# Gated linear attention feeding a top-1 mixture of experts on one core: index writes, weight splits, logits, warm products and the expert stage's order rearranged

## The chip, the core and the metric

The kernel runs on one core of one Trainium2 chip. The core has five engines with an instruction stream each: TensorE (PE, matrix products and transposes), VectorE (DVE), ScalarE (ACT), GpSimd (POOL) and SyncE (SP, which here issues most transfers). Sixteen DMA engines move data between memory and the on-chip buffers. The metric is the time of one execution in device microseconds.

## What is computed

```python
for t in range(768):                       # batch 4, 8 heads, head size 48
    state = alpha[:, :, t, :, None] * state + einsum('bhd,bhe->bhde', k_t, v_t)
    y_t = einsum('bhd,bhde->bhe', q_t, state)
x = y.transpose(0, 2, 1, 3).reshape(4, 768, 384)
logits = x @ w_gate                        # 8 experts
local = sigmoid(x @ w_local)
e = argmax(logits) if first token or local < 0.5 else expert of the token before
out = softmax(logits)[e] * (relu(x @ w1[e]) @ w2[e])     # 384 -> 1024 -> 384
```

There are 3072 tokens. Each goes through one expert alone, so the tokens of an expert are gathered by lists of indices.

## The kernel before

**Recurrence.** The tokens are cut into 24 blocks of 128 (six per sequence, the four sequences in turn), each block into two chunks of 64. Per block i, DVE runs two scans of the gates (`scan1`, tile A; `scan2`, tile sf), POOL multiplies q and k by them, PE transposes k (`kt`, kp), forms the scores (`pm`, pe), the state update (`um`, up) and the output (`ym`, y), then transposes the output (`xt`, xp) and computes the logits (`logit`, lg). DVE adds the state (`sums`, `carry`) and masks the scores; ACT copies the state (`first`, sb), kp, y (XR) and xp out of the accumulators. SP loads a, k, q three blocks ahead and v (vt) two ahead, and writes XR to memory (xd), from where experts gather tokens.

**Routing.** `route` is a generator, one per group of blocks (`SPANS`: groups of 8, 4, 8 and 4 blocks). It is stepped by `other()`, three times per block. Its DVE and PE steps find each token's expert, weight and row in the expert's list; its last steps write the rows (tile pl) to the lists in memory (ls) by indirect writes on POOL, one per block of tokens, 24 in all. A `yield` after every second write hands out two writes per call.

**Experts.** Products are made at float32 accuracy from two rounded halves: a weight is loaded raw (rw), ACT makes the high half (w1h, w2h) and POOL or DVE the rest (w1l, w2l); an expert has seven pieces of weights (three of 512 KB, four of 384 KB). `Job` is one list of tokens: load the list (li), gather the tokens (xg), transpose (tp, xh, xl), `gemm1` (h, hh, hl), `gemm2` (yp), scale (yo) and write out indirectly. Jobs a and b are the two halves of the list of expert 0: a is computed among the last blocks of the recurrence, with expert 0's weights loaded from block `W0` = 4 on, one piece per block; b is the first of the expert stage. Jobs r0 to r6 are the other seven experts, the fullest first; which expert that is, SP reads from the chip at run time (eri).

**Order.** During the recurrence each instruction is pinned behind the one traced before it on its engine (`Engine`, `keep_in_program_order`). The pin of an indirect write goes to its own register move, which is not pinned. From the end of job a on (`pinned[0] = False`) the order on each engine is chosen by the framework's scheduler.

Before the loop, PE runs `DN0` = 60 products of zeros (warm). An overflow loop for lists longer than planned stands at the end and is skipped for these inputs.

Of the kernel before, what the change touches and what calls it, by code (L numbers as in the profile page):

```python
# [51 lines left out]
DN0 = 60  # L52
# [12 lines left out]
def gla_moe(ctx, tc, akq, vw, vn, wg, w1, w2, cst, tok, out):  # L65
# [57 lines left out]
    class Weights:  # L123


        def __init__(self, e, nm, ahead=NW, lo=(1, 1, 1), defer=lambda f: f()):
            self.e, self.nm, self.ahead, self.lo, self.defer = e, nm, ahead, lo, defer
            self.raw, self.w1, self.w2 = [], [], []

        def load(self):  # L130
            n = len(self.raw)
            if n < 3:
                rw = wp.tile([128, F], F32, tag="rw", bufs=NW, name=f"rw1_{self.nm}_{n}")
                src = w1[ds(self.e, 1), :, n, :].rearrange("o p f -> p (o f)")
                y_.dma_start(rw, src)
            else:
                rw = wp.tile([128, 2, DM], F32, tag="rw", bufs=NW, name=f"rw2_{self.nm}_{n}")
                src = w2[ds(self.e, 1), :, 2 * (n - 3):2 * (n - 2), :].rearrange("o p k f -> p (o k f)")
                y_.dma_start(rw.rearrange("p k f -> p (k f)"), src)
            self.raw.append(rw)  # L140

        def steps(self):
            for n in range(7):
                while len(self.raw) < min(7, n + self.ahead):
                    self.load()
                rw = self.raw[n]
                t, b, sh = ("w1", 4, [128, F]) if n < 3 else ("w2", 6, [128, 2, DM])
                hi = wp.tile(sh, F32R, tag=t + "h", bufs=b, name=f"{t}h_{self.nm}_{n}")
                lo = wp.tile(sh, F32R, tag=t + "l", bufs=b, name=f"{t}l_{self.nm}_{n}")
                s_.copy(hi, rw)  # L150
                self.defer(lambda e=g_ if n < 3 and self.lo[n] else v_, lo=lo, rw=rw, hi=hi:
                           e.tensor_tensor(lo, rw, hi.bitcast(F32), ALU.subtract))
                if n < 3:
                    self.w1.append((hi, lo))
                else:
                    self.w2 += [(hi[:, 0, :], lo[:, 0, :]), (hi[:, 1, :], lo[:, 1, :])]
                yield

        def all(self):
            for _ in self.steps():  # L160
                pass
            return self

    class Job:
# [81 lines left out]
    with ExitStack() as ac:  # L246
# [6 lines left out]
        dz = ap.tile([128, 128], F32R, bufs=1, name="dz")  # L253
# [3 lines left out]
        v_.tensor_copy(dz, z2[:, 0:128])  # L257
# [5 lines left out]
        for j in range(2):  # L263
            sb = ap.tile([R, 2, 2, CW], F32, bufs=1, name=f"sb{j}")
            g_.memset(sb[0:64], 0.0)
            g_.memset(sb[64:112, :, 1, :], 0.0)
            SBs.append(sb)
# [98 lines left out]
        def state0(i):  # L366

            d = blk[i]
            if i < G:
                s3 = ap.tile([R, 3, HP, D], F32, tag="st", bufs=G + 1, name=f"st_{i}")  # L370
                g_.memset(s3[:, 0], 0.0)
            else:
                s3 = st["S", i % G]
            d["s3"] = s3
            first(i, 0)
# [20 lines left out]
        def sums(i):  # L396
            d = blk[i]
            s3 = d["s3"]
            n = 2 if i + G < NB else 1
            v_.tensor_tensor(s3[:, 1:1 + n], d["up"][:, 0:n], s3[:, 0].unsqueeze(1).broadcast_to([R, n, HP, D]), ALU.add)  # L400
# [37 lines left out]
        def logit(i):  # L438
            g, j, n = span[i]
# [7 lines left out]
            if j == n - 1:  # L447
                steps.append(route(g, lg))

        def route(g, lg):  # L450
# [8 lines left out]
            L = rt([128, n, E + 1], "L")  # L459
            s_.copy(L, lg[:, :, 0:E + 1])  # L460
# [5 lines left out]
            yield  # L466
# [59 lines left out]
            ix = rt([128, n], "ix", I32)  # L526
            ps = rt([128, E, n + 1], "ps")
# [3 lines left out]
            with nc.allow_low_precision(reason="whole numbers, one of them not zero"):  # L531
                v_.tensor_reduce(ix, po, AX.X, ALU.add)
            st["c"] = ps[:, :, n]
            if cb * G == T1:
                st["c"] = rt([128, E], "cm")
                v_.tensor_tensor(st["c"], ps[:, :, n], c1, ALU.max)
            if cb == NBB:
                v_.tensor_copy(cF, ps[:, :, n])
            yield
            for j in range(n):  # L540
# [3 lines left out]
                if j % 2 == 1 and cb < NBB:  # L544
                    yield
            if cb * G == T1:
                gathers.append(0)

        steps, gathers = [], []

        def other():

            flush()
            for r in list(steps):
                if next(r, 0) == 0:
                    steps.remove(r)

        for i in range(3):
# [9 lines left out]
        mids(1)  # L568
        mids(2)
# [21 lines left out]
        for _ in range(DN0):  # L591
            t_.matmul(warm[:, 0, 0:128], lhsT=dz, rhs=dz, start=True, stop=True)

        EW = Weights(FIRST, "a", 2, (0, 0, 0), later.append)
        wsteps = iter(())
# [16 lines left out]
        tr = None  # L612
        scan1(0)
        scan2(0)
        for i in range(NB + 2):
            if i + 3 < NB:
# [15 lines left out]
            if i == NB:  # L632
                st["hp"] = pp.tile([128, 2, 512], F32, tag="pe", name="hp")
            if i >= NB:
                next(work)
            other()
# [4 lines left out]
            if i < NB:  # L641
                mask(i)
            if i >= NB:
                next(work)
            other()
# [3 lines left out]
            if i + 3 < NB:  # L649
                load_q(i + 3)  # L650
                mids(i + 3)
            if 0 < i and i + 2 < NB:
                load_v(i + 2)
            if i > 1:
                logit(i - 2)
            if i >= NB:
                next(work)
            other()
            if gathers:
                if gathers[0] == 0:  # L660
                    ja.load_list()
                elif gathers[0] == 1:
                    ja.gather()
# [3 lines left out]
            if i == W0:  # L667
                wsteps = EW.steps()
            next(wsteps, None)
        while steps:  # L670
            next(work, None)
            other()
        jb.load_list()
        jb.gather()
        for _ in work:
            flush()
        flush()

        pinned[0] = False
# [19 lines left out]
        v_.tensor_scalar_mul(eri[:, 1], er[0:1], float(RS))  # L699
        both = col([128, 2, E], "both")  # L700
# [13 lines left out]
    jb.sp, jb.ps = mp, qp  # L714
    jobs = [jb]
    for r in range(NR):
        jobs.append(Job(f"r{r}", RANKS[r], None, mp, qp, 8, 2, 9, 4, ("tp", 2), (("yp",), 3)))

    def reg(q, r, top):
        return nc.values_load(eri[0:1, q, r:r + 1], engines=[ENG.SP], min_val=0, max_val=top,  # L720
                              skip_runtime_bounds_check_because="an expert number or the first row of its list")

    W = EW
    for _ in jb.trans():
        pass
    for n, j in enumerate(jobs):
        nx = jobs[n + 1] if n + 1 < len(jobs) else None
        if nx:
            nx.r0 = reg(1, n, (E - 1) * RS)
            nx.load_list()  # L730
            nx.gather()
        for _ in j.gemm1(W):
            pass
        if nx:
            Wn = Weights(reg(0, n, E - 1), nx.nm).all()
            for _ in nx.trans():
                pass
        for _ in j.gemm2(W):
            pass
        if nx:  # L740
            W = Wn


    nt = mp.tile([8, 1], F32, bufs=1, name="nt")
    gt = mp.tile([8, NOV], F32, bufs=1, name="gt")
    v_.tensor_tensor(gt, cntp.broadcast_to([8, NOV]), cc("jt", 0, 8), ALU.is_gt)
    v_.tensor_reduce(nt, gt, AX.X, ALU.add)
    tp = qp.tile([8, 2], F32, tag="tp", name="ovt")
    t_.matmul(tp[:, 0:1], lhsT=cc("tri8", 0, 8), rhs=nt, start=True, stop=True)
    t_.matmul(tp[:, 1:2], lhsT=cc("ones", 0, 8)[:, 0:8], rhs=nt, start=True, stop=True)  # L750
    cum = mp.tile([8, 2], F32, bufs=1, name="cum")
    v_.tensor_copy(cum, tp)
    ti = mp.tile([8, 1], I32, bufs=1, name="ti")
    v_.tensor_copy(ti, cum[:, 1:2])
# [150 lines left out]
```

## Time and profile before

| | us |
|---|---|
| median of three runs | 519.94 (517.18 to 526.35) |
| the profiled execution | 519.54 |
| its span, first to last instruction | 517.7 |
| PE busy in it | 451.7 (87%) |
| DVE, POOL, ACT busy | 234.0, 220.9, 166.3 |
| mean granted TensorE clock | 0.844 |

```profile
DMA  8563546846376462110172632254443545344301
GB/s 219 128 181 97 173 145 180 263 132 130 57 212 147 119 181 77 54 33 1 28 235 67 187 107 90 76 167 116 150 113 96 198 127 171 104 158 141 106 2 36
q1 hardware_dynamic: 27300, 53.63, 36.9%
```

The first two rows cut the span into 40 slices of 12.9 us: the mean busy share of the DMA engines in tenths, and what they moved. Matmul spans are modelled and overlap, so a busy PE is not PE at its peak. The order of the stages in time: recurrence to about 236 us, job b from 266, the seven experts from about 288 to 509.

### The profile page before, as it was taken

The numbers are of one execution on the slowest core, as the hardware profiler recorded it, in microseconds if no ns is written. First come the engines' busy times: TensorE is split into PE (matmuls) and PEld (weight loads), VectorE is DVE, ScalarE is ACT, GpSimd is POOL, SyncE is SP. The second block draws the span as 40 slices with busy tenths as digits, with TensorE's granted clock in tenths as the row PEclk, the third lists the DMA queues.
The fourth block names the chain that finished last, engine by engine and source line by source line (L and its number), as shares of the span: only waits on it lengthen the run. The fifth ranks groups of instructions, "written<-read, shape, count | busy, mean of one in ns | idle before, by whom it ended". The sixth has DMA issues, their size and how long they took to land.

```text
span 517.7 us, 10609 instructions
## 1 busy us (share of the span) xinstructions
PE 451.7 (87%) x4147; PEld 410.3 (79%) x4147; DVE 234.0 (45%) x406; ACT 166.3 (32%) x342; POOL 220.9 (43%) x276
## 2 busy tenths in 40 slices
PE   8879599796596999998349899999989999998993
PEld 8668488685485887887339689999879999997993
DVE  4763256974396454433314433326235253533521
ACT  0232244533253333332014332243242342424310
POOL 8633032525838252123460835255353464345303
PEclk9995555958597555699759989999999999999998
DMA  8563546846376462110172632254443545344301
GB/s 219 128 181 97 173 145 180 263 132 130 57 212 147 119 181 77 54 33 1 28 235 67 187 107 90 76 167 116 150 113 96 198 127 171 104 158 141 106 2 36
DMA packets 35354, 64.77 MB, mean 125 GB/s; under 512 B 9821, under 2 KB 17758, under 8 KB 35302
## 3 DMA queue, kind: packets, MB, share of 16 engines
q1 hardware_dynamic: 27300, 53.63, 36.9%
q0 software_dynamic: 6272, 10.09, 6.5%
q8 instruction: 33, 0.54, 0.5%
q10 hardware_dynamic: 1730, 0.36, 0.4%
q14 instruction: 19, 0.16, 0.1%
HBM read 54.51 MB, written 10.11 MB: 125 GB/s over the span
## 4 chain that ended last, share of the span: by engine, by line
PE 52%; DMA 15%; issue 15%; POOL 8%; DVE 5%; ACT 3%; SPq 1%; POOLq 0%; ACTq 0%; DVEq 0%
PE yp_r L79 12%; PE y L79 11%; PE h_r L79 9%; PE up L79 4%; PE lg L79 4%; PE pe L79 3%; POOL w1l_r L79 3%; DMA rw_r<-w 3%; PE kp L79 3%; DMA xg_r<-xd,li_r 2%; DMA rw_a<-w 2%; PE xp L79 2%; POOL out L79 1%; POOL ls L79 1%; PE hp L79 1%
## 5 line engine op out<-in xcount | busy, mean ns | idle before, releaser
L79 POOL TENSOR_TENSOR w1l_r<-rw_r,w1h_r 128x1024 fp32r<-128x1024 f32 x21 | 50.1, 2402 | 55.6 <-ACT w1h_r L79 55.4
L79 PE MATMUL yp_r<-w2h_r,hh_r 128*128 128x384 f32 (+4 forms) x200 | 68.0, 343 | 2.5 <-ACT hh_r L79 2.4
L79 PE MATMUL yp_r<-w2l_r,hh_r 128*128 128x384 f32 (+4 forms) x200 | 67.7, 341 | 0.0
L79 DVE SCALAR_TENSOR_TENSOR hl_r<-h_r,hh_r 128x384 fp32r<-128x384 f32 (+5 forms) x56 | 32.8, 598 | 70.5 <-ACT hh_r L79 70.3
L79 PE MATMUL yp_r<-w2h_r,hl_r 128*128 128x384 f32 (+4 forms) x200 | 64.4, 340 | 0.0
L79 PE MATMUL h_r<-xh_r,w1h_r 128*128 128x384 f32 (+5 forms) x168 | 60.0, 359 | 0.2 <-DVE hl_r L79 0.2
L79 PE MATMUL h_r<-xl_r,w1h_r 128*128 128x384 f32 (+5 forms) x168 | 59.7, 356 | 0.0
L79 PE MATMUL h_r<-xh_r,w1l_r 128*128 128x384 f32 (+5 forms) x168 | 59.2, 354 | 0.0
L79 POOL TENSOR_TENSOR k<-k,sf 112x512 f32<-112x512 f32 x24 | 29.1, 1212 | 63.9 <-DVE sf L79 58.7
L79 DVE TENSOR_TENSOR w2l_r<-rw_r,w2h_r 128x768 fp32r<-128x768 f32 x28 | 32.5, 1160 | 49.7 <-ACT w2h_r L79 49.3
L79 POOL DMA_INDIRECT out<-yo_r,li_r x25 | 27.3, 1093 | 54.9 <-DVE yo_r L79 52.2
L79 ACT CAST w2h_r<-rw_r 128x768 fp32r<-128x768 f32 x28 | 23.4, 837 | 74.0 <-DMA rw_r<-w 46.6
L79 PE MATMUL y<-sb,q 112*64 112x96 f32 x384 | 34.1, 326 | 11.7 <-ACT sb L79 11.7
L79 ACT ACTIVATE hh_r<-h_r 128x384 fp32r<-128x384 f32 (+5 forms) x56 | 28.6, 524 | 47.3 <-PE h_r L79 47.3
L79 PEld LDWEIGHTS y<-sb,q 112*64 112x64 f32 x384 | 26.6, 189 | 19.5 <-ACT sb L79 13.3
L79 POOL DMA_INDIRECT xg_r<-xd,li_r x25 | 28.9, 1158 | 30.4 <-DMA li_r<-ls 24.4
L79 DVE TENSOR_TENSOR_SCAN sf<-a,z 112x520 f32<-112x520 f32 x24 | 34.0, 1415 | 15.5 <-POOL k L79 15.4
L79 ACT COPY sb<-st 48x192 f32<-48x192 f32 x96 | 33.7, 351 | 19.3 <-POOL st L79 9.2
L79 PEld LDWEIGHTS yp_r<-w2h_r,hh_r 128*128 128x128 f32 (+4 forms) x200 | 36.4, 182 | 4.3 <-ACT hh_r L79 3.8
L79 DVE TENSOR_TENSOR st<-up,st 112x384 f32<-112x384 f32 (+1 forms) x24 | 12.5, 520 | 60.5 <-PE up L79 60.5
L79 PE MATMUL y<-vt,pq 64*64 64x48 f32 x768 | 38.3, 269 | 0.0
L79 PEld LDWEIGHTS y<-vt,pq 64*64 64x64 f32 x768 | 34.9, 184 | 4.3 <-issue 3.1
(169 smaller groups left out, 878.2 us busy)
## 6 DMA issues: line engine op xcount, KB each, us to landing
rw_r<-w SPq DMA_DIRECT2D x21, 512.0 KB, 5.2
rw_r<-w SPq DMA_DIRECT2D x28, 384.0 KB, 3.2
a<-akq SPq DMA_DIRECT2D x24, 227.9 KB, 4.2
k<-akq SPq DMA_DIRECT2D x24, 224.0 KB, 4.0
q<-akq SPq DMA_DIRECT2D x24, 224.0 KB, 3.9
vt<-vn SPq DMA_DIRECT2D x24, 192.0 KB, 3.6
xd<-XR SPq DMA_DIRECT2D x24, 192.0 KB, 1.9
vt<-vn SPq DMA_DIRECT2D x24, 96.0 KB, 3.9
```

The lines of the kernel that those rows point to most:

```text
L79: r = f(*a, **k)
```

## The change

- `DN0` becomes 48 products of 240 columns. In each block, `logit` adds `DN` = 4 products of zeros with 240 columns, into unused columns of the logits' accumulator.
- The logits come out transposed: 32 columns of gate weights are the stationary operand and the 128 tokens move; four blocks (32 rows each) fill one tile, which a new generator `logits` copies, transposes and copies to the group's L.
- `route` writes one row per `yield`, with one call of three left out: two per block while the loop runs, faster once it has drained.
- Expert 0's pieces are loaded from block 2 on and split at every second block from block 4 on.
- For the last group, `fast` makes the part of job b's list that this group fills by comparing row numbers and small products on PE, adds it to the part that is already in memory, and gathers from that; the writes of the group come after.
- The memset of a is issued one iteration later, the state's memset and the adds of zeros of the first four blocks are dropped, the copy of en moves from POOL to ACT, deferred work is flushed after the routing step.
- The whole expert stage is pinned: pieces of the next expert's weights stand at fixed places of `gemm1` and `gemm2`, with one of three first-layer subtractions on POOL and two on DVE; transposes are spread over `gemm2`; the overflow count is made in job r0's place of the loop.

```diff
-DN0 = 60
+DN0 = 48
+DN = 4
...
+        def split(self, p):
+            n = self.order[p]
+            rw = self.raw[p]
...
+            s_.copy(hi, rw)
+            self.defer(lambda: (g_ if n in self.pool else v_).tensor_tensor(lo, rw, hi.bitcast(F32), ALU.subtract))
...
-        dz = ap.tile([128, 128], F32R, bufs=1, name="dz")
+        dz = ap.tile([128, 256], F32R, bufs=1, name="dz")
...
-            g_.tensor_copy(d["end"], end)
+            s_.copy(d["end"], end)
...
-            if j == 0:
-                st["lg"] = pp.tile([128, n, 16], F32, tag="lg", name=f"lg_{g}")
+            if o == 0:
+                st["lg"] = pp.tile([128, 368], F32, tag="lg", name=f"lg_{c}")
             lg = st["lg"]
             for k in range(3):
-                t_.matmul(lg[:, j, 0:E + 1], lhsT=xx[:, k, :], rhs=wgs[:, k, 0:E + 1], start=(k == 0), stop=(k == 2))
+                t_.matmul(lg[32 * o:32 * (o + 1), 0:128], lhsT=wgs[:, k, :], rhs=xx[:, k, :], start=(k == 0), stop=(k == 2))
+            for _ in range(DN if i + 2 < NB else 0):
+                t_.matmul(lg[:, 128:368], lhsT=dz[:, 0:128], rhs=dz[:, 0:240], start=True, stop=True)
...
+            lc = ap.tile([128, 128], F32, tag="lc", bufs=1, name=f"lc_{c}")
+            s_.copy(lc, lg[:, 0:128])
+            yield
+            lt = pp.tile([128, G, 32], F32, tag="lg", name=f"lt_{c}")
+            t_.transpose(lt.rearrange("p b e -> p (b e)"), lc, ident)
...
+            s_.copy(grp[g][:, j:j + G], lt[:, :, 0:E + 1])
...
-                if j % 2 == 1 and cb < NBB:
+                if cb < NBB and not (drained[0] and j % 2 == 0):
                     yield
+                    if j % 2 == 1 and not drained[0]:
+                        yield
...
+        def fast(pl, xf, n, ca):
...
+                v_.tensor_scalar(hot, rows, xf[:, j:j + 1], None, ALU.is_equal)
+                for s in range(ns):
+                    t_.matmul(lp[s], lhsT=hot[:, s * P:(s + 1) * P], rhs=pf[:, j, :], start=(j == 0), stop=(j == n - 1))
...
+                v_.tensor_tensor(li.bitcast(I32)[:, s, 1:3], lf[:, s, :], lp[s][:, 1:3], ALU.add)
+            for _ in jb.gather():
+                pass
...
-                mids(i + 3)
+            if i + 2 < NB:
+                mids(i + 2)
...
-            if i == W0:
-                wsteps = EW.steps()
-            next(wsteps, None)
+            w = i - W0
+            if w == -2:
+                EW.load()
+                EW.load()
+            if 0 <= w < 14 and w % 2 == 0:
+                EW.split(w // 2)
+                EW.load()
...
-        pinned[0] = False
...
+    Ws = [EW] + [Weights(lambda r=r: reg(0, r, E - 1), f"r{r}", (0, 3, 4, 1, 2, 5, 6), (0,)) for r in range(NR)]
+    for _ in range(NW):
+        Ws[1].load()
...
+        for f, _ in enumerate(j.gemm1(W)):
+            if n and f < 2:
+                piece(W, 5 + f)
+            if nx:
+                if 1 <= f:
+                    next(gt, None)
+                if f in (3, 5, 7):
+                    piece(Wn, (f - 3) // 2)
...
+        for q, _ in enumerate(j.gemm2(W)):
+            if nx and q in (0, 2):
+                piece(Wn, 3 + q // 2)
+            for _ in range(at_.count(q)):
+                next(tr)
...
+    pinned[0] = False
```

`spread` gives the steps of `gemm2` after which a transpose of the next job stands; `piece` splits a piece and issues the next load.

More of the change, by code (lines that the diff above doesn't have):

```diff
@@ L123, in gla_moe, with __init__ @@
     class Weights:
-        def __init__(self, e, nm, ahead=NW, lo=(1, 1, 1), defer=lambda f: f()):
-            self.e, self.nm, self.ahead, self.lo, self.defer = e, nm, ahead, lo, defer
-            self.raw, self.w1, self.w2 = [], [], []
+        def __init__(self, e, nm, order, pool=(), defer=lambda f: f()):
+            self.e, self.nm, self.order, self.pool, self.defer = e, nm, order, pool, defer
+            self.raw = []
+            self.w1, self.w2 = [None] * 3, [None] * 8
         def load(self):
-            n = len(self.raw)
+            if len(self.raw) == len(self.order):
+                return
+            n = self.order[len(self.raw)]
+            e = self.e() if callable(self.e) else self.e
+            self.e = e
@@ L139, in load @@
-                y_.dma_start(rw.rearrange("p k f -> p (k f)"), src)
+                y_.dma_start(rw.rearrange("p k f -> p (k f)"),
+                             w2[ds(e, 1), :, 2 * (n - 3):2 * (n - 2), :].rearrange("o p k f -> p (o k f)"))
             self.raw.append(rw)
[L142 to L162, printed above, removed]
+        def split(self, p):
+            n = self.order[p]
+            rw = self.raw[p]
+            t, b, sh = ("w1", 4, [128, F]) if n < 3 else ("w2", 6, [128, 2, DM])
+            hi = wp.tile(sh, F32R, tag=t + "h", bufs=b, name=f"{t}h_{self.nm}_{n}")
+            lo = wp.tile(sh, F32R, tag=t + "l", bufs=b, name=f"{t}l_{self.nm}_{n}")
+            s_.copy(hi, rw)
+            self.defer(lambda: (g_ if n in self.pool else v_).tensor_tensor(lo, rw, hi.bitcast(F32), ALU.subtract))
+            if n < 3:
+                self.w1[n] = (hi, lo)
+            else:
+                m = 2 * (n - 3)
+                self.w2[m], self.w2[m + 1] = (hi[:, 0, :], lo[:, 0, :]), (hi[:, 1, :], lo[:, 1, :])
@@ L264, in gla_moe @@
             sb = ap.tile([R, 2, 2, CW], F32, bufs=1, name=f"sb{j}")
-            g_.memset(sb[0:64], 0.0)
-            g_.memset(sb[64:112, :, 1, :], 0.0)
+            g_.memset(sb, 0.0)
             SBs.append(sb)
@@ L369, in state0 @@
             if i < G:
-                s3 = ap.tile([R, 3, HP, D], F32, tag="st", bufs=G + 1, name=f"st_{i}")
-                g_.memset(s3[:, 0], 0.0)
-            else:
-                s3 = st["S", i % G]
-            d["s3"] = s3
-            first(i, 0)
+                d["s3"] = ap.tile([R, 3, HP, D], F32, tag="st", bufs=G + 1, name=f"st_{i}")
+            else:
+                d["s3"] = st["S", i % G]
+                first(i, 0)
         def first(i, c):
@@ L530, in route @@
             v_.tensor_tensor(po, ps[:, :, 0:n].rearrange("p e b -> p b e"), ob, ALU.mult)
-            with nc.allow_low_precision(reason="whole numbers, one of them not zero"):
-                v_.tensor_reduce(ix, po, AX.X, ALU.add)
+            v_.tensor_reduce(xf, po, AX.X, ALU.add)
             st["c"] = ps[:, :, n]
@@ L590, in gla_moe, with dense @@
         warm = pp.tile([128, 2, 512], F32, tag="pe", name="warm")
[L591 to L595, printed above, removed]
+        def dense(n):
+            for _ in range(n):
+                t_.matmul(warm[:, 0, 0:240], lhsT=dz[:, 0:128], rhs=dz[:, 0:240], start=True, stop=True)
+        dense(DN0)
+        EW = Weights(FIRST, "a", (0, 1, 2, 3, 4, 5, 6), (), later.append)
         ja = Job("a", PART1, FIRST * RS, m1, pp, 2, 1, 8, 2, ("rt", 1), (("up", "y"), 1), 1 + T1 * 128, later.append)
@@ L642, in gla_moe @@
                 mask(i)
+            other()
             if i >= NB:
                 next(work)
-            other()
             if 0 < i <= NB:
@@ L655, in gla_moe @@
                 logit(i - 2)
+            other()
             if i >= NB:
                 next(work)
-            other()
             if gathers:
@@ L662, in gla_moe @@
                 elif gathers[0] == 1:
-                    ja.gather()
+                    steps.append(ja.gather())
                 elif gathers[0] == 3:
@@ L666, in gla_moe @@
                 gathers[0] += 1
-            if i == W0:
-                wsteps = EW.steps()
-            next(wsteps, None)
+            w = i - W0
[5 more added lines that the diff above has]
+                EW.load()
         while steps:
+            other()
             next(work, None)
[L672 to L677, printed above, removed]
-        pinned[0] = False
         def col(shape, nm, dt=F32):
@@ L699, in gla_moe, with reg @@
         v_.tensor_scalar_mul(eri[:, 1], er[0:1], float(RS))
+        jobs = [jb]
+        for r in range(NR):
+            jobs.append(Job(f"r{r}", RANKS[r], None, None, None, 8, 2, 9, 4, ("tp", 2), (("yp",), 3)))
+        def reg(q, r, top):
+            return nc.values_load(eri[0:1, q, r:r + 1], engines=[ENG.SP], min_val=0, max_val=top,
+                                  skip_runtime_bounds_check_because="an expert number or the first row of its list")
+        Ws = [EW] + [Weights(lambda r=r: reg(0, r, E - 1), f"r{r}", (0, 3, 4, 1, 2, 5, 6), (0,)) for r in range(NR)]
+        for _ in range(NW):
+            Ws[1].load()
+        for _ in work:
+            flush()
+        flush()
         both = col([128, 2, E], "both")
@@ L713, in gla_moe, with spread @@
     qp = ctx.enter_context(tc.tile_pool(name="qp", bufs=2, space=PSUM))
[L714 to L723, printed above, removed]
+    for j in jobs:
+        j.sp, j.ps = mp, qp
+    def spread(k, n):
+        return [(t + 1) * n // (k + 1) for t in range(k)]
     for _ in jb.trans():
@@ L727, in gla_moe, with piece @@
         nx = jobs[n + 1] if n + 1 < len(jobs) else None
+        W, Wn = Ws[n], Ws[n + 1] if nx else None
+        def piece(w, p):
+            w.split(p)
+            if len(w.raw) < 7:
+                w.load()
+            elif n + 2 < len(Ws) and w is Wn:
+                Ws[n + 2].load()
+            elif Wn is not None and w is W:
+                Wn.load()
         if nx:
@@ L730, in gla_moe @@
             nx.load_list()
-            nx.gather()
-        for _ in j.gemm1(W):
-            pass
[L734 to L754, printed above, removed]
+            gt = nx.gather()
+        for f, _ in enumerate(j.gemm1(W)):
[6 more added lines that the diff above has]
+                    piece(Wn, (f - 3) // 2)
+        if n == 1:
+            nt = mp.tile([8, 1], F32, bufs=1, name="nt")
+            gr = mp.tile([8, NOV], F32, bufs=1, name="gr")
+            v_.tensor_tensor(gr, cntp.broadcast_to([8, NOV]), cc("jt", 0, 8), ALU.is_gt)
+            v_.tensor_reduce(nt, gr, AX.X, ALU.add)
+            tp = qp.tile([8, 2], F32, tag="tp", name="ovt")
+            t_.matmul(tp[:, 0:1], lhsT=cc("tri8", 0, 8), rhs=nt, start=True, stop=True)
+            t_.matmul(tp[:, 1:2], lhsT=cc("ones", 0, 8)[:, 0:8], rhs=nt, start=True, stop=True)
+            cum = mp.tile([8, 2], F32, bufs=1, name="cum")
+            v_.tensor_copy(cum, tp)
+            ti = mp.tile([8, 1], I32, bufs=1, name="ti")
+            v_.tensor_copy(ti, cum[:, 1:2])
+        at_ = spread(nx.ns, 4 * j.ns) if nx else []
+        tr = nx.trans() if nx else None
+        for q, _ in enumerate(j.gemm2(W)):
[3 more added lines that the diff above has]
+                next(tr)
+        for _ in tr or ():
+            pass
+    pinned[0] = False
     NT = nc.values_load(ti[0:1, 0:1], min_val=0, max_val=NOV,
```

65 lines of the change are left out of this document (47 added, 18 removed).

## The prediction

> **What bounds the kernel now.** I read the page's slices and clock first, then the chain of work that ended last, then the same stretches by window, then each engine's own timeline where TensorE (PE) stood idle.
>
> ```profile
> PEclk9995555958597555699759989999999999999998
> 23.41 3.42 PE y L79 x46
> 72.56 3.36 PE y L79 x48
> 75.92 1.38 PE lg L79 x6
> 77.29 1.48 PE up L79 x16
> 78.77 0.94 PE kp L79 x4
> 79.71 1.06 PE pe L79 x32
> 80.78 0.83 PE xp L79 x3
> 72.56:81.61 9.05, 9.05 (x111) 7.76 (x113) 5.66 (x9) 3.85 (x8) 2.60 (x4) 0.50 0.68 198
> 90.20:95.30 5.10, 5.10 (x111) 4.41 (x110) 4.59 (x7) 3.41 (x8) 2.78 (x4) 1.00 0.82 242
> 150.20:156.00 5.80, 5.80 (x114) 5.06 (x113) 5.59 (x15) 2.61 (x9) 3.13 (x4) 1.00 0.80 224
> 215.30:220.90 5.60, 5.60 (x112) 4.86 (x111) 1.83 (x5) 2.65 (x7) 0.75 (x1) 0.94 0.11 38
> 35.35 0.38 PE L79 MATMUL y<-sb,q 112*64 112x96 f32 x2
> 228.42 0.88 PE L79 MATMUL y<-sb,q 112*64 112x96 f32 x16
> ```
>
> (A window row: stretch, length, busy us of PE, weight loads, VectorE (DVE), ScalarE (ACT), GpSimd (POOL), granted clock, DMA share, GB/s.) In the first half the granted clock is 0.5 about half of the time. The six pieces of the chain from 72.56 us are one block of the recurrence at clock 0.50; they add up to 9.05 us, the whole block, so PE bounds it. Three blocks at full clock take 5.10, 5.80 and 5.60, mean 5.5, and PE fills those too. Before 28 us the page shows 1.00 only because no change is recorded yet: block 0's y took 3.42 us, the half-clock price. From block 2's y at 35.3 us to block 23's, the last, at 228.4 us are 193.1 us for 21 blocks, 9.2 each (the last two rows). The clock, and the idle gaps that drop it, are what the first half costs.
>
> ```profile
> 35.02:38.43 3.41, 0.70 (x5) 0.35 (x4) 3.09 (x5) 1.33 (x4) 3.24 (x5) 1.00 0.98 252
> 53.91 6.50 DMA rw_a<-w
> 60.43 1.05 ACT w1h_a L79
> 55.50:63.40 7.90, 2.18 (x37) 1.44 (x30) 1.90 (x2) 2.88 (x7) 0.00 (x0) 0.50 0.60 199
> 99.87:103.28 3.41, 0.97 (x35) 0.66 (x27) 3.22 (x8) 2.60 (x7) 2.56 (x6) 1.00 0.97 248
> 121.56 1.18 POOL L79 DMA_INDIRECT ls<-pl,ix  x1 [2.66 <-DVE ix L79]
> 132.78 0.97 POOL L79 DMA_INDIRECT ls<-pl,ix  x1 [0.31 <-issue]
> 133.75 1.21 POOL L79 TENSOR_TENSOR k<-k,sf 112x512 f32<-112x512 f32 x1
> 124.80:135.00 10.20, 0.00 (x0) 0.00 (x0) 0.56 (x2) 0.00 (x0) 7.18 (x9) 0.62 0.63 92
> 160.10:164.50 4.40, 0.04 (x2) 0.03 (x1) 0.61 (x3) 0.00 (x0) 3.89 (x6) 0.64 0.88 179
> ```
>
> Each drop of the clock follows a gap. At 35 us POOL waits for a load of a before the memset that ACT needs. At 54 us ACT stands on a weight split whose load has not landed until 60.4, with y's state copies behind it, and PE works 2.2 of 7.9 us; before 100 us the same again. At 121.6 us eight index writes (first and last quoted) run back to back, 12.2 us, ahead of block 13's product k, and PE stands 10.2 us; the second group, four writes, costs 4.4.
>
> ```profile
> 247.43 0.19 DVE L79 TENSOR_REDUCE ix<-po 128x4 int32<-128x32 f32 x1
> 255.18 3.09 DMA li_b<-ls
> 259.22 5.17 DMA xg_b<-xd,li_b
> 268.07 0.96 PE L79 MATMUL h_b<-xh_b,w1h_a 128*128 128x240 f32 x3 [0.60 <-ACT xh_b L79]
> 236.00:268.00 32.00, 14.88 (x91) 13.07 (x90) 9.04 (x43) 3.80 (x10) 15.72 (x18) 0.77 0.31 91
> 288.00:301.30 13.30, 10.24 (x45) 8.74 (x44) 5.75 (x8) 4.49 (x7) 11.69 (x8) 0.87 0.64 186
> 301.30:509.40 208.10, 203.65 (x1133) 193.88 (x1132) 80.27 (x123) 69.02 (x113) 86.02 (x59) 1.00 0.39 118
> 509.40:517.70 8.30, 0.00 (x0) 0.00 (x0) 0.60 (x1) 0.00 (x0) 1.57 (x2) 0.71 0.19 48
> ```
>
> The last logits end at 236.0. From there to job b's first product at 268.07 PE works 14.9 of 32 us: index, write, list, gather follow each other through memory. From 301.3 on PE is busy 203.65 of 208.1 us at full clock; there is little to win there.
>
> **Does denser PE work raise the clock?** Rows that decide it:
>
> ```profile
> L79 PE MATMUL warm<-dz 128*128 128x128 f32 x60 | 13.1, 416 | 2.1 <-DVE z L79 2.1
> 24.78:28.19 3.41, 3.41 (x50) 3.04 (x48) 0.00 (x0) 1.18 (x3) 0.74 (x3) 1.00 0.03 5
> 270.53:273.95 3.42, 3.42 (x18) 3.42 (x17) 0.00 (x0) 0.17 (x1) 0.50 0.32 108
> 273.95:277.36 3.41, 0.00 (x0) 0.00 (x0) 1.00 0.38 106
> 237.12 1.03 PE hp L79 x9
> ```
>
> The 60 warm-up products of 128 columns take 13.1 us, 0.218 each, 590 columns of a full array per us, and left the clock at half (block 0's y). Products of 240 columns (h_b, the stretch from 270.53: 16 whole ones and two cut by its edges) start 0.21 apart at half clock, 1140 columns per us, and in the next stretch the clock was at 1.00. So pace in columns, not being busy, seems to count. As an estimate I weigh each product by its share of the array and count a float32 one twice (up: 16 of 96 columns, two side by side, in 1.48 us is 1.9 ns a column against 0.9 for h_b). Then y and up make 500 and 900 per us; the stretch 24.78 to 28.19, two thirds of y and all of up, made 620, and its successor ran at full clock. So the border lies between 590 and 620 over some 3.4 us. A block at half clock makes 480 on average and only rarely 620. The change adds 4 products of 240 columns in front of up: 0.85 us at 1140, up's 1.48 us at 900, and some 1.1 us of y or logits at up to 500 make about 800 over 3.4 us, once in every block. I expect the clock back within about one block of each drop.
>
> The Trainium skill, "TensorE: Matmul & The Clock Gate", section "What's actually happening", says that one busy window of about 3.4 us releases the full clock and an idle one takes it. The trace agrees on idle (0.97 us busy of 3.41 at 99.87, then half clock), and not on busy: PE was busy throughout 72.56 to 81.61 and stayed at 0.50. By that rule alone the zero products add nothing; that is the first rival.
>
> **The change part by part.**
> - Warm-up: 48 of 240 columns at 0.21 are 10.2 us instead of 13.1, so kp of block 0 (14.95 us in the before) can come up to 2 us sooner; POOL's first k ends at 13.0. I take 1.5; bounds 0 to 3.
> - Zero products per block: 4 x 0.114 (hp, 9 in 1.03) = 0.46 at full clock, 4 x 0.21 = 0.85 at half, all on PE's path.
> - Logits with 32 weight columns and 128 moving ones instead of 128 and 9: not in the trace. The nearest rows bound it: now six in 1.38 at half clock; by up's float32 pace (0.185 for 96 columns) six would be 1.48; cheaper if the small weights hide. I take no difference. The copy, one transpose and one copy per four blocks add about 0.2 of PE and 0.7 of ACT; ACT is busy 2.6 to 3.9 of a block, so that hides.
> - en to ACT (24 x 0.46 off POOL, about 0.2 each on ACT), state memsets and zero adds of the first four blocks dropped, memset of a one iteration later: they take the 35 us gap (2.7 us) away. ACT has cover as above.
> - Weight loads two blocks ahead, one split every second block: the gaps at 55 and 100 us go (PE idle 7.90 - 2.18 = 5.7 and 3.41 - 0.97 = 2.4 us). On SP's queue stand behind these loads the next block's a, k, q and v; a load of 512 KB is 5 us of latency but 2 us of DMA at 250 GB/s every second block, and a, k and q are issued over a block ahead. DMA share was 0.80 to 0.82 in two hot blocks, so this fits with little room: at 1155 KB a block plus half a weight piece, 6 us needs 235 GB/s; 242 was moved at 0.82.
> - Index writes: two per block instead of up to six. In the trace the old six-per-block code still ran eight in one row, ahead of k of the block, so what runs is not the order of the loop alone: a write is taken as soon as it is ready. If they now spread, 2.5 us a block beside POOL's 2.5 to 3.1, nothing shows. If they run in one row, it is again up to 10.2 and 4.4 us. Behind them on POOL wait q and k, behind those PE. I take 6 us for both groups; bounds 0 and 14.6.
> - Half clock after gaps: two drops at such gaps, each about one block at 9.9 (9.05 + 0.85) instead of 6; part of it is the gap's own shadow, so I take 6 us in all.
> - A hot block: 5.5 + 0.46 = 5.96, taken as 6.0. Then 21 blocks are 126 + 6 + 6 = 138 instead of 193.1.
> - Half list on chip: from ix at 247.6, about 1 us for the extra logits step, then three small DVE rows, four comparisons near hl_a's 0.41, the small products, three small DVE rows: 3.3 us; the gather can start at 252.3 instead of 259.2. Behind it on POOL now stand the four writes, so job r0's list comes no sooner. Gain 6.9; bounds 4 and 9. So 32.0 becomes 25.1.
> - Fixed order in the expert stage: PE idles 13.30 - 10.24 = 3.1 and 208.10 - 203.65 = 4.5 us there now. POOL loses two of three weight subtractions (2.40 each), DVE gains them at about 1.22; DVE is busy 80 of 208 us. r0's first weights are the tight spot: its fourth piece is loaded only after the first is split, behind the gathers on POOL. I take 241.4 - 3.4 = 238 for 268 to 509.4; bounds 234 and 250.
> - Tail 8.3 unchanged; the overflow count moved to job 1 lies beside other work already.
>
> **The sum.** 35.3 - 1.5 = 33.8, then 138, then 7.6 (block 23's y to the last logits, 228.4 to 236.0), 25.1, 238, 8.3: 450.8 us of span. The run's own time is 519.54 for a span of 517.7, 1.8 more, and the median 519.94 is 0.4 above that: 453.
>
> **The rivals.**
> - The clock does not follow the zero products (they are zeros, or busy alone counts as the page has it). Then 15 half-clock blocks pay 0.75 to 0.85 each, 12 us, six hot ones 3, and the removed gaps give 11: 35.3 to 228.4 stays about 197 and the time is about 33.8 + 197 + 7.6 + 25.1 + 238 + 8.3 + 2.2 = 512. For it: the warm-up's zeros raised nothing. Against: they were at 590 per us. 11%.
> - The clock comes up but the writes run in one row and loads tighten: gaps of 14.6 rather than 6, a drop more, blocks at 6.8: 143 + 15 + 10 = 168 instead of 138, so 483. For it: eight in a row above. 17%.
> - Slower: in the fixed order weights become the bound of the expert stage. A piece is loaded (5.2 us), split by ACT (1.05) and subtracted (POOL 2.40); were only one in flight, 7 x 6.25 = 44 us per expert against PE's 30, 14 us for each of seven jobs, 98 in all, 551. It decides once pieces take over 30/7 = 4.3 us each; with three buffers in flight it is 8.65/3 = 2.9. 8%.
>
> ```profile
> rw_r<-w SPq DMA_DIRECT2D x21, 512.0 KB, 5.2
> L79 POOL TENSOR_TENSOR w1l_r<-rw_r,w1h_r 128x1024 fp32r<-128x1024 f32 x21 | 50.1, 2402 | 55.6 <-ACT w1h_r L79 55.4
> ```
>
> **How the numbers follow.** Forecast 453 (433 to 478) 62%: low end with blocks at 5.6 and no gap (118 + 2 instead of 138, two off the list), high end with a drop or two more. Second rival 478 to 500, 17%; below 433, 2%; first rival 11%, slower 8%. The range 433 to 500 leaves out two in ten. A measurement here tells 2% from nothing, 509.5 to 530.3 being the same: faster 0.82, same 0.10 (nearly all of the first rival), slower 0.08.
>
> **What would show it.** The clock row: 0.5 only in stretches of one or two slices after 30 us; block starts 5.6 to 6.2 apart; no weight wait of ACT among the long ones; POOL's writes in pairs with q or k between; job b's first product about 25 us after the last logits; PE still over 95% busy from the first r job on. Wrong if the clock stays at 0.5 over many blocks that hold zero products, or if DMA waits hold blocks above 6.8.

## The result and the profile after

The changed kernel takes 461.05 us (median of four, 457.97 to 461.98) against 521.15 (517.18 to 526.35) in the same series: a ratio of 0.886, 95% interval 0.878 to 0.893. The forecast was 453 in a range of 433 to 500. The profiled execution took 461.34 us, its span 459.5, mean granted clock 0.956 instead of 0.844. The page of the kernel after, PE's busy tenths and the granted clock in 40 slices of 11.5 us:

```profile
PE   7699999949979988882999799999999999999992
PEclk9799999996998999996899899999999999999997
```

The long fives of before are gone. The drops that are left are short: one in the second slice, behind the warm-up, and the next in the tenth, behind the 4 of PE in the ninth. Stretches of the kernel after by window (columns as in the prediction):

```profile
30.50:36.60 6.10, 6.09 (x114) 4.94 (x113) 4.47 (x7) 2.98 (x8) 2.41 (x3) 1.00 0.93 279
93.00:107.30 14.30, 7.59 (x116) 5.99 (x115) 5.29 (x8) 3.66 (x12) 10.52 (x11) 0.80 0.67 135
98.10:104.10 6.00, 0.02 (x1) 0.00 (x0) 0.00 (x0) 0.00 (x0) 5.19 (x6) 0.80 0.80 115
107.30:115.70 8.40, 8.40 (x117) 6.88 (x116) 6.07 (x16) 3.69 (x11) 2.67 (x5) 0.72 0.56 115
188.70:216.30 27.60, 16.30 (x108) 14.71 (x108) 10.69 (x55) 2.83 (x10) 9.55 (x11) 0.90 0.25 74
237.20:450.90 213.70, 210.83 (x1173) 202.19 (x1171) 104.77 (x146) 75.07 (x121) 66.04 (x52) 0.99 0.42 125
```

A hot block takes 6.1 us and PE fills it. Blocks 12 and 13 (14.30 and 8.40 us) hold PE idle for 6 us while POOL alone works, and then the half clock that follows. POOL's timeline there, and PE's waits in the recurrence and after it:

```profile
91.28 1.43 POOL L80 DMA_INDIRECT ls<-pl,ix  x1 [1.50 <-DVE st L80]
93.02 1.11 POOL L80 DMA_INDIRECT ls<-pl,ix  x1 [0.30 <-issue]
...
100.86 0.98 POOL L80 DMA_INDIRECT ls<-pl,ix  x1 [0.30 <-issue]
101.85 1.19 POOL L80 TENSOR_TENSOR q<-q,A 112x512 f32<-112x512 f32 x1
```

```profile
PE kp L80 <- POOL a L80: 7.1, 2, 6.1
...
PE h_b L80 <- ACT xh_b L80: 7.9, 1, 7.9
PE ovt L80 <- DVE nt L80: 2.8, 1, 2.8
```

The index writes do not come in pairs: all eight (first two and last shown) still run in one row, now ahead of q and not of k. The pin goes to the write's register move, so the loop's spacing does not bind the write itself.

The stages of the profiled executions that are compared below, in us of span. The borders are the first product y of blocks 2 and 23, the end of the last logits, job b's first product and the end of the last yp of job r6; "half" sums the time at half clock between the two y, from the trace's changes of the clock, and "idle" PE's gaps over 0.8 us there.

| kernel | to y(2) | y(2) to y(23) | half | idle | to logits' end | to job b | to last yp | rest |
|---|---|---|---|---|---|---|---|---|
| before | 35.3 | 193.1 | 133.0 | 26.5 | 7.6 | 32.1 | 241.3 | 8.4 |
| forecast | 33.8 | 138 | | | 7.6 | 25.1 | 238 | 8.3 |
| after | 30.5 | 150.3 | 13.6 | 9.3 | 7.9 | 27.6 | 234.5 | 8.7 |
| after, no zero products | 30.7 | 146.2 | 20.5 | 14.9 | 7.9 | 27.2 | 234.3 | 8.8 |
| before + zero products | 36.4 | 183.8 | 81.8 | 24.1 | 7.6 | 31.4 | 244.0 | 8.1 |
| before + 32-row logits | 35.8 | 159.4 | 30.7 | 29.8 | 7.9 | 33.5 | 241.9 | 8.0 |
| after, old logits, no zero products | 30.0 | 155.7 | 54.5 | 15.4 | 7.6 | 27.1 | 234.4 | 8.8 |
| the same + small zero products | 35.3 | 156.1 | 27.3 | 9.3 | 7.6 | 26.5 | 234.4 | 8.7 |
| after, writes held in place | 29.9 | 141.3 | 0.0 | 3.5 | 7.9 | 27.2 | 234.0 | 8.7 |
| the last version | 28.5 | 139.5 | 3.4 | 5.7 | 7.9 | 27.3 | 230.7 | 8.8 |

In these traces the clock is either full or half, so each run's mean clock and span give its whole time at half clock, 2 x (1 - clock) x span, also where no trace was kept. The time ahead of a trace's first change counts as full in it. For the profiled execution of before it gives 162 us, 133 of them between the two y. Between runs of the kernel before the time varies by 9 to 25 us within a series, so a difference of a few us against another series is read together with its stage.

### The profile page after: what moved, and what is told of

Read it like the earlier page. It is cut to its first block, busy times and chain, and to the rows that moved or that the text cites. A ratio compares the mean times of both kernels' runs of the same rounds, so it can differ in the third digit from the quotient of the medians.

```text
span 459.5 us, 10789 instructions
## 1 busy us (share of the span) xinstructions
PE 416.8 (91%) x4245; PEld 375.8 (82%) x4245; DVE 258.7 (56%) x436; ACT 167.4 (36%) x366; POOL 173.3 (38%) x233
## 4 chain that ended last, share of the span: by engine, by line
PE 49%; issue 9%; POOL 5%; DVE 3%; DMA 2%; ACT 1%; POOLq 0%; SPq 0%; ACTq 0%
PE h_r L80 18%; PE yp_r L80 18%; PE y L80 3%; PE lg L80 2%; POOL out L80 2%; PE tp_r L80 1%; PE hp L80 1%; DMA ls<-pl,ix 1%; PE up L80 1%; POOL w1l_r L80 1%; PE yp_a L80 1%; POOL xg_r L80 1%; DMA rw_r<-w 1%; PE yp_b L80 1%; POOL ls L80 1%
## 5 line engine op out<-in xcount | busy, mean ns | idle before, releaser
L80 POOL DMA_INDIRECT out<-yo_r,li_r x25 | 27.2, 1089 | 116.5 <-DVE yo_r L80 112.6
L80 PE MATMUL yp_r<-w2h_r,hl_r 128*128 128x384 f32 (+4 forms) x200 | 68.0, 340 | 0.0
L80 POOL DMA_INDIRECT xg_r<-xd,li_r x25 | 28.7, 1148 | 38.7 <-DMA li_r<-ls 28.9
L80 DVE TENSOR_TENSOR_SCAN A<-a,z 112x520 f32<-112x520 f32 x24 | 29.6, 1232 | 20.1 <-POOL a L80 20.1
L80 POOL TENSOR_TENSOR q<-q,A 112x512 f32<-112x512 f32 x24 | 28.4, 1183 | 31.3 <-DVE A L80 26.1
L80 PEld LDWEIGHTS yp_r<-w2l_r,hh_r 128*128 128x128 f32 (+4 forms) x200 | 36.6, 183 | 0.3
L80 PEld LDWEIGHTS yp_r<-w2h_r,hl_r 128*128 128x128 f32 (+4 forms) x200 | 36.5, 183 | 0.3
L80 DVE TENSOR_TENSOR w2l_r<-rw_r,w2h_r 128x768 fp32r<-128x768 f32 x28 | 34.5, 1232 | 2.9 <-ACT w2h_r L80 1.2
L80 PE MATMUL y<-sb,q 112*64 112x96 f32 x384 | 29.6, 264 | 4.3 <-ACT sb L80 4.1
L80 PEld LDWEIGHTS h_r<-xl_r,w1h_r 128*128 128x128 f32 x168 | 31.6, 188 | 2.2 <-DVE xl_r L80 0.3
L80 PEld LDWEIGHTS h_r<-xh_r,w1l_r 128*128 128x128 f32 x168 | 31.6, 188 | 2.0
L80 PEld LDWEIGHTS h_r<-xh_r,w1h_r 128*128 128x128 f32 x168 | 31.5, 188 | 2.0
```

The source lines that it names most:

```text
L80: r = f(*a, **k)
```

## The experiments

### The zero products

Theory of the prediction: they bring the clock back. Taken out of the kernel after:

```diff
-DN = 4
+DN = 0
```

> The changed kernel without the four zero products per block (the warm-up stays). Theory (a column pace of about 600 per us over 3.4 us brings the clock back, and the zero products supply it): after each gap the clock stays at 0.5 for several blocks, as before; some ten blocks at 9.05 instead of 5.7 us cost 34 us, the missing products save 20 x 0.46 = 9: 486 us (470 to 505). Rival (the gaps that were removed made the difference, zero products do nothing): only the 9 us are saved, 452.

Measured: 456.67 us (455.5 to 458.3), no slower than with them, and near the 452 of the rival. The theory fell. The clock row of this kernel, a hot block, and the second half of the stretch at half clock behind the writes:

```profile
PEclk9689999977979899985999899999999999999997
```

```profile
30.75:36.23 5.48, 5.47 (x111) 4.41 (x110) 4.50 (x7) 2.98 (x9) 2.41 (x3) 1.00 0.91 277
103.70:107.20 3.50, 3.50 (x46) 2.70 (x38) 3.46 (x6) 2.33 (x8) 2.27 (x3) 0.51 0.48 30
```

In the recurrence the clock comes back after 3.4 to 7 us without them, and a hot block that PE fills is 5.5 us instead of 6.1. The other way round, the kernel before with the same four products behind each block's logits:

```diff
...
+            for _ in range(DN if i + 2 < NB else 0):
+                t_.matmul(lw[:, 128:368], lhsT=dz[:, 0:128], rhs=dz[:, 0:240], start=True, stop=True)
```

> The kernel before, with nothing but the four zero products of 240 columns added to each block. Theory: all gaps stay (25 us of PE idle between blocks 2 and 23), the clock is back about one block after each, blocks take 6.0: 126 + 25 + 20 = 171 instead of 193 us, 498 in all (485 to 510). Rival (zero products do not count): 15 half-clock blocks pay 0.85 more, 532.

Measured: 520.1 us, ratio 1.010 (0.998 to 1.021): neither theory. Half clock falls from 133 to 82 us, the stretch by 9.3 us in the profiled execution, the fastest of ten. Over all runs the effect is small (117 to 177 us of half clock in the whole run, 144 to 184 for the kernel before in the same series), the products cost time in each block, and nothing is gained. Its clock, and two stretches:

```profile
PEclk9885569997558599999769899999999999999998
```

```profile
40.00:74.10 34.10, 28.63 (x302) 24.65 (x302) 10.52 (x15) 9.06 (x20) 6.48 (x11) 0.50 0.42 122
121.90:156.00 34.10, 26.69 (x314) 22.59 (x314) 16.25 (x32) 8.05 (x22) 14.76 (x20) 0.50 0.39 100
```

With four zero products in every block the old kernel stays at 0.50 for 34 us twice. Part of that is PE's gaps, but the second stretch goes on for 27 us after its gap has ended at 129.3. So something else in the changed kernel must bring the clock back.

### The parts of the change

Each write held behind the last traced POOL instruction, so that it keeps its place in the loop:

```diff
-                apart(lists, g_.indirect_dma_start(
+                at_pool = next(p for p in reversed(nc.cur_bb.bb.instructions) if p.engine == ENG.Pool)
+                with tc.issue_after(at_pool):
+                    apart(lists, g_.indirect_dma_start(
...
```

> The changed kernel with each index write held in the place where the loop hands it out (its register move queued behind the last POOL instruction), so that they really stand two per block between q and k. Theory: the gap of 8 us before block 13's y, the 1.6 of the second group and the half-clock blocks behind them go, 449 us (445 to 453), clock 1.00 throughout from 25 to 200 us. Rival: POOL with 5.1 of 6.1 us busy delays q or k in every block that holds writes, 458 to 462.

Measured: 451.1 us (450.5 to 452.1). As expected. POOL's timeline now alternates, and no half clock is left between y(2) and y(23):

```profile
90.71 1.43 POOL L80 DMA_INDIRECT ls<-pl,ix  x1 [1.50 <-DVE st L80]
92.16 1.57 POOL L80 TENSOR_TENSOR q<-q,A 112x512 f32<-112x512 f32 x1
93.89 1.76 POOL L80 DMA_INDIRECT ls<-pl,ix  x1 [0.16 <-issue]
95.68 1.20 POOL L80 TENSOR_TENSOR k<-k,sf 112x512 f32<-112x512 f32 x1
```

```profile
29.90:171.20 141.30, 132.97 (x2395) 108.16 (x2394) 119.76 (x190) 71.00 (x194) 72.22 (x81) 1.00 0.72 187
```

With the zero products taken out as well (`DN = 0`):

> Index writes held in their places and no zero products per block. Theory: what the zero products do is bring the clock back after gaps; without gaps a block at full clock makes about 800 columns per us by itself and holds the clock, so the products are only a cost: 449 - 9 = 440 us (437 to 446). Rival: small gaps remain and drop the clock for several blocks, 455 to 475.

Measured: 450.5 us (446.2 to 452.0), between the two expectations. Between y(2) and y(23) 13.7 us of half clock come back, where the run with zero products had none; the stretch is as long (141.6 against 141.3). Without the gap at the writes the zero products are worth about what they cost.

The half list read from memory again, list and gather after the last writes:

```diff
-            if cb == NBB:
-                fast(pl, xf, n, ca)
...
+        jb.load_list()
+        for _ in jb.gather():
+            pass
```

> The changed kernel with job b's list read back from memory after the last writes, as before (the comparison and small products on chip left out). Theory: the last logits to job b's first product take 32 us again instead of 27.6, 465 to 467 us. Rival: job r0's weights and list end last anyway and hide it, 461.

Measured: 466.2 us (464.9 to 466.4), 5.2 more than the kernel after, 4.6 of them in its stage: last logits to job b 32.2 us instead of 27.6. Confirmed.

The order of the expert stage left to the scheduler:

```diff
+    pinned[0] = False
     mp = ctx.enter_context(tc.tile_pool(name="mp", bufs=2))
```

> The changed kernel with the order of the expert stage left to the framework's scheduler (the traced order is the changed kernel's). Theory: the fixed order is worth what job b's first product to the last yp lost against before, 241.4 - 234.5 = 7 us less some 3 of half clock: 464 to 468 us. Rival: PE was full already, no difference, 459 to 463.

Measured: 466.2 us (464.0 to 468.5), 5.1 more, of which its stage has 4.1: job b to the last yp 238.6 us instead of 234.5. Confirmed.

Expert 0's weights loaded from block 4 on and split one per block, as before:

```diff
-            if w == -2:
+            if w == 0:
...
-            if 0 <= w < 14 and w % 2 == 0:
-                EW.split(w // 2)
-                EW.load()
+            if 0 <= w < 7:
+                EW.split(w)
+                if w + 2 < 7:
+                    EW.load()
```

> The changed kernel with expert 0's weights loaded from block 4 on, just ahead of their use, and split one piece in every block, as before. Theory: ACT waits for loads again, gaps of about 5.7 and 2.4 us come back with a half-clock block behind each: 470 us (466 to 476). Rival: the zero products and the lead make it harmless, 460 to 463.

Measured: 472.8 us (471.4 to 474.5), 11.7 more, as expected, and all of it between y(2) and y(23) (162.0 us against 150.3). Of the two gaps expected one is back, longer than before (this kernel by window, PE idle, and ACT's split, which waits for its load):

```profile
43.10:50.90 7.80, 0.02 (x1) 0.00 (x0) 2.02 (x2) 3.01 (x8) 0.00 (x0) 0.61 0.79 256
47.81 1.04 ACT L80 CAST w1h_a<-rw_a 128x1024 fp32r<-128x1024 f32 x1 [8.34 <-DMA rw_a<-w]
```

The warm-up with 48 products of 128 columns instead of 240:

```diff
-                t_.matmul(warm[:, 0, 0:240], lhsT=dz[:, 0:128], rhs=dz[:, 0:240], start=True, stop=True)
+                t_.matmul(warm[:, 0, 0:128], lhsT=dz[:, 0:128], rhs=dz[:, 0:128], start=True, stop=True)
```

> The changed kernel whose 48 warm-up products have 128 columns instead of 240, one look at the clock. Theory (pace of columns counts): 48 x 0.218 = 10.5 us of busy PE at 590 columns per us leave the clock at half, no change is recorded before the recurrence has begun; in the changed kernel it was at full from 6.1 us on. Rival (being busy counts): full clock from about 6 us, as with 240 columns. Time within 3 us of the changed kernel.

Measured, in a single run: 455.9 us, 5.2 less than the kernel after and so outside the 3 us expected. For the clock the theory held: the trace's first change of the clock, to full, comes at 16.2 us; with 240 columns it comes at 6.1 and the clock falls again at 16.4. The windows ahead of 16.2 and 16.4, first of the kernel after, then of this one:

```profile
13.00:16.40 3.40, 1.54 (x38) 1.14 (x38) 2.49 (x5) 0.28 (x2) 1.52 (x3) 1.00 1.07 220
```

```profile
13.00:16.20 3.20, 3.20 (x53) 2.58 (x52) 1.58 (x2) 0.53 (x1) 2.01 (x3) 1.00 0.98 218
```

(Ahead of a trace's first change, 16.2 in the second, its rows show 1.00 whatever the clock.) The wide warm-up is over at 9.7 us, PE then works only in part while it waits for block 0, and the clock goes; the narrow one lasts until 12.7 and hands over to block 0 without a break. Block 2's y comes at 28.9 instead of 30.5 us.

### The logits

New theory: the new logits move 128 columns per product where the old ones moved 9, and that brings the clock back. In the kernel after without zero products, the old form:

```diff
-                t_.matmul(lg[32 * o:32 * (o + 1), 0:128], lhsT=wgs[:, k, :], rhs=xx[:, k, :], start=(k == 0), stop=(k == 2))
+                t_.matmul(lg[:, j, 0:E + 1], lhsT=xx[:, k, :], rhs=wgs[:, k, 0:E + 1], start=(k == 0), stop=(k == 2))
...
```

> Kernel after, without the zero products and with the logits as before (tokens as the loaded weights, 9 moving columns instead of 128). New theory: it is the 128 moving columns of the new logits, three products in each block, that bring the clock back. Then the stretches at half clock after each gap become as long as before (before: 51, 14, 14 and 55 us; without zero products alone: 3.4 to 10 us), 60 to 110 us of the recurrence stand at half clock instead of 20.7, and with blocks of 9.0 instead of 5.5 us there the time is 473 to 493 us against 456.7 without the zero products alone. Rival: only the gaps decide how long the clock is low. Then half-clock time stays near 20 us and the time is 452 to 460 us.

Measured: 483.4 us, its four runs from 465.5 to 498.7 with mean clocks of 0.91 down to 0.82; with the new logits the four had 0.94 to 0.95. The median lies in the expected range and the direction is the theory's, but the size scatters: the whole run holds 85 to 182 us of half clock, against 42 to 55 with the new logits. The fastest of the four, the one with a trace, has 54.5 us of it in the recurrence, a little under the 60 expected, and its 465.5 us lie between the two expectations. Its clock row, and a stretch after the second writes:

```profile
PEclk9799998965975599996799899999999999999997
```

```profile
133.00:163.00 30.00, 29.57 (x363) 25.15 (x363) 17.08 (x22) 10.45 (x29) 11.14 (x15) 0.50 0.60 149
```

PE is busy 29.57 of 30 us and the clock stays at 0.50. The kernel before with the new logits alone:

> Kernel before with the 32-row logits alone, no zero products, gaps as they were. New theory (the logits' 128 moving columns bring the clock back): half-clock time between the first products y of blocks 2 and 23 falls from 133 us to below 60, the gaps (26.5 us) stay, and the time is 480 to 500 us. Rival (gaps decide, logits do not matter): half-clock time above 110 us, the time is 514 to 526 us.

Measured: 490.4 us against 513.7 for the kernel before beside it, ratio 0.964 (0.951 to 0.977). Confirmed: the gaps stay (29.8 us), half clock falls from 133 to 31 us, and in the whole run it is 66 to 87 us in the four runs against 132 to 178 in the seven of the kernel before. Its clock, and the stretch behind the writes, where the gap ends at 125.6 and 0.50 at 131.6:

```profile
PEclk9988689899598999995698899999999999999998
```

```profile
121.30:124.70 3.40, 0.00 (x0) 0.00 (x0) 0.00 (x0) 0.00 (x0) 3.09 (x5) 0.51 0.78 176
124.70:128.10 3.40, 2.49 (x39) 2.09 (x39) 2.51 (x2) 1.23 (x3) 3.34 (x5) 0.50 0.18 41
128.10:131.60 3.50, 3.50 (x47) 2.94 (x48) 3.29 (x11) 0.67 (x2) 1.25 (x4) 0.50 0.27 70
```

Is it the columns, or the new order and waits around the logits? The old logits kept, without the wide zero products, and behind them three products of zeros in the shape of the new logits:

```diff
...
+            for k in range(3 if i + 2 < NB else 0):
+                t_.matmul(lw[0:32, 256:384], lhsT=dz.bitcast(F32)[:, 0:32], rhs=dz.bitcast(F32)[:, 0:128], start=True, stop=True)
...
```

> The kernel of the old logits without the 240-column zero products, and behind the logits of each block three float32 products of zeros in the shape of the new logits (32 loaded columns, 128 moving). If what brings the clock back is the columns that such small products move, whatever they compute and however little of the array they fill, half-clock time of the recurrence falls to 10 to 30 us and the mean clock of every run is 0.93 to 0.96 (old logits without these: 0.82 to 0.91 in four runs; new logits: 0.94 to 0.95); the extra products cost 22 x 0.5 to 0.85 us, so 465 to 478 us, with a scatter of some 5 us. Rival: it is the new order and the waits around the new logits. Then the clock stays scattered between 0.82 and 0.91 and the time between 475 and 515 us.

Measured: 468.1 us (465.0 to 470.5), mean clock 0.93 to 0.95 in all four runs, half clock 27.3 us, and 48 to 65 us in the whole run, where none of the four runs without these products has under 85. Confirmed for the clock: three float32 products of 32 loaded and 128 moving columns per block bring it back, zeros or not, without the new order around the logits. They are extra work, 1.49 us per block at half clock, and in time they gain 15 us on the median without them and nothing on its fastest run (465.5):

```profile
117.72 1.49 PE L80 MATMUL lg<-dz 128*32 128x128 f32 x6
```

### The version built from these

Writes held, two zero products per block, warm-up of 128 columns, and the overflow count's two products one job later than their operand:

```diff
-DN = 4
+DN = 2
...
             v_.tensor_reduce(nt, gr, AX.X, ALU.add)
+        if n == 2:
...
```

> The kernel after with each list write held in its place, two zero products per block instead of four, warm-up products of 128 columns instead of 240, and the products that count the overflow tiles one job later than their operand. From the runs so far: 450.5 to 451.1 us with the writes held, about 3 us less since the clock is up after the warm-up and does not fall again at 16 us, 2.8 us less for the wait ahead of the overflow count and 1 to 2 for the half clock behind it: 443 to 446 us. Rival: the low clock only moves elsewhere, 449 to 452 us.

Measured: 446.2 us (444.3 to 448.1), ratio to before 0.875 (0.866 to 0.884), faster than both kernels, the median just above the 443 to 446 expected. From the first r job on, PE has no idle time left:

```profile
224.50:433.80 209.30, 209.30 (x1173) 200.49 (x1171) 104.75 (x145) 75.38 (x121) 65.79 (x52) 1.00 0.42 128
```

## Why the prediction came out as it did

The time fell in the range and the clock did what was forecast, but the main reason given was wrong. That the forecast held for the clock was luck: the change carried, beside the zero products, another part that did their work.

- **Does denser PE work raise the clock?** Yes, but the step "the change adds 4 products of 240 columns ... I expect the clock back within about one block of each drop" names the wrong part. Without them the changed kernel is no slower, and alone in the old one they gain nothing; where they lower the time at half clock (13.6 against 20.5 us, none against 13.7 with the writes held), they cost about what that saves. Most of it is done by the new logits, which the prediction gave "no difference". That was right for PE's time (six records in 0.84 us before and after, last rows of this section) and left out what they do to the clock: 31 instead of 133 us at half clock, some 20 us of time, alone in the old kernel. The weighting failed: it counted a product by the share of the array that it fills, and so 32 of 128 columns as a quarter.

  Nor did the border between 590 and 620 follow from the prediction's own rows (below). By its weights the stretch from 24.78 holds 2112 columns (32 x 48 x 0.25, 8 x 96 x 0.375 and 8 x 96 x 0.5, twice; half of up's records load 64 columns), which is the 620 per us. The y of 72.56 holds as many (16 x 96 x 0.4375 and 32 x 48 x 0.25, twice) in the same 3.4 us, where the prediction has 500, and the clock stayed at half.

```profile
24.88 1.95 PE L79 MATMUL y<-vt,pq 64*64 64x48 f32 x32
26.75 1.55 PE L79 MATMUL up<-vt,kk 128*48 128x96 f32 x16
...
72.49 1.55 PE L79 MATMUL y<-sb,q 112*64 112x96 f32 x16
73.97 1.95 PE L79 MATMUL y<-vt,pq 64*64 64x48 f32 x32
```

- **First rival (512).** Its condition, a clock that does not follow the zero products, is close to what the two runs on them show; its price was wrong, since it kept the 15 blocks at half clock, from which the new logits brought the clock back.
- **Hot block 6.0:** 6.1. The block without zero products was right (5.5); with them, a block that PE fills is 0.65 us longer (6.13 against 5.48), not 0.46.
- **Index writes, 6 us:** "if they now spread" did not come true. Holding them gains 9.0 us of the recurrence (150.3 to 141.3), gap and half clock together, most of the 12.3 us by which the 138 was too low.
- **Weight loads ahead:** 8.1 us of gaps were forecast; undone, they cost 11.7, with the half clock behind them.
- **Start, 1.5 us:** 4.8. No run took this gain apart; the narrow warm-up adds 1.6.
- **Half list, 6.9 us:** 4.5 in its stage (32.1 to 27.6), 5.2 by the run without it. The gather started even sooner than forecast, 13.9 us behind the last logits (202.6) instead of 16.3, but PE then waits 7.9 us for xh_b and starts job b at half clock. What held xh_b is not tested; the profile names the landing of job a's output write, which stands behind the four index writes on POOL (issued at 210.59):

```profile
215.34 0.82 ACT L80 CAST xh_b<-tp_b 128x360 fp32r<-128x360 f32 x2 [18.95 <-DMA out<-yo_a,li_a]
```

- **Expert stage, 3.4 us:** 6.8, of which the fixed order is 4.1 (238.6 to 234.5). That "the overflow count moved to job 1 lies beside other work already" was wrong: PE waits 2.8 us for its operand nt. One job later the stage is 3.3 us shorter (234.0 with the writes held, 230.7 in the last version), the wait and the half clock behind it together.
- **Second and third rival:** the writes did run in one row, as the second said, but loads did not tighten. Weights did not bound the experts: PE is busy 210.83 of 213.70 us.

What stays open: which measure of PE's work the clock follows. The rows allow an estimate, but it does not hold: products of 240 columns start 0.11 apart at full clock, 2100 columns per us, and the three logits' 384 columns take 0.84 us, 460 per us. If a float32 column thus counted some four times, and a small stationary operand as a full one, a block's logits would make 1500 and the zero products 960, which is the order of their effect. But the same count gives y, with 1536 float32 columns in every block of both kernels, four times the logits' figure, and y left the clock at half in the kernel before (72.56 to 81.61). Only the narrow warm-up varied the columns alone: full products of 240 columns raised the clock within 4 us, those of 128 columns did not in 10.5. No run varied the type or the loaded width alone. (The rows are of the kernel after; the last one is the old logits in the kernel before.)

```profile
186.82 0.28 PE L80 MATMUL hp<-xl_a,w1h_a 128*128 128x240 f32 x1
...
187.38 0.28 PE L80 MATMUL hp<-xh_a,w1h_a 128*128 128x240 f32 x1
187.82 0.84 PE L80 MATMUL lg<-xx,wgs 128*32 128x128 f32 x6
```

```profile
230.30 0.84 PE L79 MATMUL lg<-wgs,xx 128*128 128x9 f32 x6
```

## What to carry to other kernels

Where PE is busy and the granted clock stays at half, look at which products move few columns, and try the operands swapped so that the long side moves: here it cost the same PE time and took 100 us off the half clock. Before adding filler work, run the kernel without it and the old kernel with it; a clock that rises is no proof that the filler raised it. Check in the trace that an instruction spaced out in the program is spaced out on its engine: a pin on the write's register move did not hold the write.

## What was not expected of the hardware

- A PE that works almost without a break can stay at half clock: 29.57 of 30.00 us busy at 0.50 with the old logits. The Trainium skill, "TensorE: Matmul & The Clock Gate", section "What's actually happening", has one busy window of about 3.4 us release the clock. The kernels with new logits, which in the recurrence come back after 3.4 to 10 us, come near to that; this row does not, and the measurement decides.
- The kernels with old logits and no products in the new shape scatter: the one of this row by 33 us between runs, the one before by 9 to 25 us in its series, with 240-column zero products by 21. Every kernel with the new logits, or with three products in their shape, stays within 8 us. What makes the clock return at another time from run to run is not shown.
- A full clock raised too early is lost again: raised at 6.1 us it fell at 16.4; raised at 16.2, it stayed until the writes at 98 us.
